# First two token segments of the MLP on whole float32 weights, with the two-part weights made later

## The chip, the cores and the metric

One core of one Trainium2 chip runs the whole program. The metric is the device time in microseconds of one execution. Three runs of the kernel before gave 595.78, 596.35 and 597.09 us; the median, 596.35 us, is the time before.

## The reference, cut to what matters

```python
state = 0                                       # one 48x48 state for each of 4 batches x 8 heads
for t in range(768):                            # gated linear attention
    state = alpha[t][:, None] * state + outer(k[t], v[t])
    y[t] = q[t] @ state
x = y as (3072 tokens, 384)
h = x @ w_in                                    # 384 -> 2048
P = a[0] + a[1]*h + a[2]*h**2 + a[3]*h**3
Q = 1 + abs(b[0])*abs(h) + abs(b[1])*h**2
out = (P / (Q + 1e-6)) @ w_out                  # 2048 -> 384
```

All inputs and the output are float32, except that both weight matrices arrive as float64 words, which the kernel itself turns into float32.

## The kernel before, in words

**Attention.** The 3072 tokens are cut into 12 segments of 256 tokens; a segment is two chunks of 128. Each chunk has two pieces (four heads each), so there are 48 pieces. Gates go through scans on VectorE (`suffix`, L389; `prefix`, L404), products on GpSimd (L418, L422), scores on TensorE (`sc_mm`, L447), evacuation on ScalarE (L456), mask on GpSimd (L460), output and state update on TensorE (`attn_mm`, L490 and L510). The output of a chunk, transposed, is the MLP's input x: ScalarE writes its rounded part (`x_hi`, L535) and VectorE the rest (`x_lo`, L540).

**MLP.** Its columns are cut into 8 units of 256 features. One *job* is one unit of one segment: 96 jobs, numbered u. The first 16 jobs belong to segments 0 and 1 (`NB0 = 2`): units 0 to 5 of segment 0 (u = 0 to 5), the same of segment 1 (6 to 11), then units 6 and 7 of each (12 to 15). From u = 16 on a segment's 8 jobs follow one another. A job does the first product (`mlp_in`, L565, into one of three PSUM banks), the rational function (ScalarE L572 to L595, GpSimd L581, VectorE L585 `t2`, L589, L599, L602, L608), the split of its result g into a rounded part gh (ScalarE, L611) and the rest gl (L615: VectorE for u below 8, GpSimd after), and the second product (`mlp_out_hi`, L626; `mlp_out_lo`, L636) into PSUM banks that collect a segment's output. The product of job u waits for g of job u - 3, whose bank it takes.

**Products in parts.** TensorE multiplies in the type float32r, whose operands are rounded. To keep the accuracy, each operand is a rounded part plus the rest, and three products are added: hi x hi, hi x lo, lo x hi. So a job's first product is 18 matmuls of 256 columns and its second 12 of 384.

**Weights.** There are 16 weight blocks ("keys"): a w_in and a w_out block for each unit. Each arrives as 768 KB of float64 words (`load_w`). ScalarE takes the absolute value of the high words (`join_abs`, L229), VectorE does three integer steps (`join_sign` L234, `join_low` L238, `join` L244), which leave the float32 block in a buffer of the ring wr; ScalarE rounds it (`split_hi`, L253), and the rest is taken from it (`split_lo`, L260) on VectorE for units 0 to 3 and on GpSimd for units 4 to 7. The first product of a job waits for `split_lo` of its w_in block.

**What sets the order.** Every step is registered with an engine, a cost and the steps that it needs; the planner's costs only served a search. The program is written out in the order of the list `ORDER`, a compressed permutation of the steps, and each engine runs its own steps strictly in that order. The planner's costs of the matrix products (1.08 us for half of `mlp_in`, 0.72 us for half of `mlp_out_hi`) are the same before and after.

Of the kernel before, what the change touches and what calls it, by code (L numbers as in the profile page):

```python
# [12 lines left out]
F32 = mybir.dt.float32  # L13
# [9 lines left out]
class Plan:  # L23
# [30 lines left out]
    'c-jTQ17IC65CG7-OD>n>Z)=BkUfbEWZQHhO+qP}nwr$(C-<t`cFcOBsR2T)(Au^1GVK5OKguplehz1iV3PgpNFrI>8',  # L54
    'Gz7scSPH`-28@ANFbx#Mh7m9xmcU$?1j}FoY=L>O80NzQ*bb{;Hf)5Iuo^bNbXWs(U@c6f888`Ez#`ZSQ(!ABhlQ{U',
    'w!scK4eJ46IqigXkP$Y)3W@{qVGW&v&9IW<!ag_*YiSiF27>*tj&{RpiU%8M4;+BwkO|gPD%eC@=m>0Ao9QTQpaif(',
    'ZKq=}iMG-X3WH*h1a{F*+D759o6f-*$N^{J0;Gn6u!l~<71*gJ(=K%g&ckzc0;)g+yigY*AsnDfP!=x3UV5cos%!98',
    'U4?yA8{Vnc>KGlSG>{1L!x2gfIpHWJgO-pMl0$b$2Pq&Iq=%Hy2r|G=RRA(WaVQACR6oc9x#5q>3LW6L0==L9D%5Y(',
    'LCOZ%;W)ilAJifGr^-PjeS)UYN3~m>p~#x_Cv}PTD5V9?(`OZ=E!+dGPf`?ZAez2F55WWLQ*@DTKy)3fPm|F%;fpE{',
    'XG!#Z_^K+vJGe}R-~;ScS177JM|a_y+NZv&!Vp8>f*&eGSA^?O1f0$TURQ!UP!#gQBM8-%A%T7mF?E=J47VX4)PeNc',  # L60
    'pw;0zgO1R3L1PI>r~|qlJb+9(u}-9`0^<|NsOy8r%(^5r0E<a<7VR*WPO7WHTZpYoK{6dz3qFI=5Kjj%xo!wkDTU6e',
    'Q|jkXP`83N@B&^!DqTpY)>U<39Y+_{)gitvqO0jLPy^EF8al1cri<z7x+bL4we?fDLD_XJsG}oe4qaRaVNU%Ta_Pnp',
    '2}|gjItn&{k~+7prAz6b&|Ei#x;h@V(Dn2mh>Ll2OPx>G*RLQx=GUcl9Q+Gq^i@(AfPYX{x7PRQ3pCI@bvfNeU!zaZ',
    'Q1{Y}bb0*|n!#w@M}LOAx;c!|fUR@^-CMWSEnuwfulwp>&`w{caIBy^!T?=SBevIJ7!@n&4mtu`!%eEJJL*VKMYn;k',
    '&_p-ZKcJ~@3*&S%{T({#e!3k@)Zbvd?yTFxK%D?5>A8B44#q6lMbFcN^#t7mGT?9MrswOPkPy4;$$E$;oT3xqP`yz1',
# [71 lines left out]
TB = 3  # L137
# [6 lines left out]
def tile_gla_then_rational_mlp(ctx, tc, q, k, v, alpha, w_in, w_out, ca, cb, out):  # L144
# [413 lines left out]
    def h_of(u):  # L558
        return bank(u % 3)
# [420 lines left out]
```

## Time and profile before

| what | value |
|---|---|
| median of three runs | 596.35 us |
| the profiled execution's own time | 596.56 us |
| its span, first to last instruction | 594.9 us |
| TensorE busy | 537.8 us (90% of the span) |
| VectorE busy | 501.2 us (84%) |
| ScalarE busy | 472.8 us (79%) |
| GpSimd busy | 389.2 us (65%) |
| mean granted TensorE clock | 0.970 |

In the profile PE is TensorE, PEld its weight loads, DVE VectorE, ACT ScalarE, POOL GpSimd and SP the queue that issues the DMAs. Busy time is the union of an engine's instructions; records of neighbours on DVE overlap by some hundredths of a microsecond. "L585" is a line of the kernel. Since busy shares are means over the span, the span has to be cut into stretches; the marks used here are the starts of `t2` (L585), the first VectorE step of each job.

### The profile page before, as it was taken

How to read it: one execution, taken by the hardware profiler on the slowest of the kernel's cores; microseconds unless marked ns; L12 is line 12 of the kernel's file. 1: busy time of each engine (PE TensorE's matmuls, PEld its weight loads, DVE VectorE, ACT ScalarE, POOL GpSimd, SP SyncE). 2: the span in 40 equal slices, each digit the busy share in tenths (PEclk: the TensorE clock that was granted, in tenths of full speed). 3: DMA queues.
4: the chain of work that ended last, by engine and by line, in shares of the span. 5: the costliest groups of instructions: out<-in, count | busy, mean ns of one | idle time of the engine just before them, and what ended most of it. 6: DMA issues, size and time to landing. Idle time of an engine off the chain costs nothing.

```text
span 594.9 us, 14103 instructions
## 1 busy us (share of the span) xinstructions
PE 537.8 (90%) x5362; PEld 502.8 (85%) x5362; DVE 501.2 (84%) x782; ACT 472.8 (79%) x803; POOL 389.2 (65%) x422
## 2 busy tenths in 40 slices
PE   3965765989989999999999999999999999999995
PEld 2644655878879999999999999899999999999994
DVE  4379999999999989998887989999899788758872
ACT  3555775767968988989898988999997987878882
POOL 4543454658787778777766676787767586655562
PEclk9986889889999999999999999999999999999998
DMA  9998431233325334344412444344402000000000
GB/s 170 216 363 327 56 39 23 35 45 49 53 32 127 48 67 84 51 66 70 83 24 57 81 91 72 49 76 81 77 29 42 14 28 2 2 28 1 28 2 32
DMA packets 179979, 41.91 MB, mean 70 GB/s; under 512 B 169408, under 2 KB 172480, under 8 KB 179904
## 3 DMA queue, kind: packets, MB, share of 16 engines
q1 hardware_dynamic: 179904, 40.94, 34.9%
q8 instruction: 44, 0.72, 0.5%
q14 instruction: 31, 0.25, 0.1%
HBM read 36.18 MB, written 4.72 MB: 69 GB/s over the span
## 4 chain that ended last, share of the span: by engine, by line
PE 72%; DVE 12%; SPq 5%; ACT 4%; DMA 4%; issue 2%; DVEq 0%; ACTq 0%
PE ps L565 31%; PE ps L626 19%; PE ps L636 10%; PE ps L490 6%; PE ps L447 5%; SPq L331 2%; SPq L356 2%; DMA wo_words<-in_moe_w_out_dram 2%; DVE wo_words L238 1%; DVE t L599 1%; DVE ps L602 1%; DMA wr<-in_alpha_dram 1%; DVE t L608 1%; DVE t L585 1%; PE ps L510 1%
## 5 line engine op out<-in xcount | busy, mean ns | idle before, releaser
L565 PE MATMUL ps<-x,wi 128*128 128x256 f32 x1728 | 231.3, 289 | 22.8 <-DVE t L608 10.7
L565 PEld LDWEIGHTS ps<-x,wi 128*128 128x128 f32 x1728 | 220.9, 195 | 32.0 <-DVE t L608 13.5
L626 PE MATMUL ps<-wo,gh 128*128 128x384 f32 x768 | 158.0, 343 | 8.9 <-ACT gh L611 5.1
L581 POOL TENSOR_TENSOR qm<-qm,ah 128x512 f32<-128x512 f32 x96 | 127.9, 1334 | 57.5 <-ACT qm L578 56.6
L615 POOL TENSOR_TENSOR gl<-t,gh 128x512 fp32r<-128x512 f32 x88 | 117.1, 1332 | 54.2 <-ACT gh L611 26.3
L626 PEld LDWEIGHTS ps<-wo,gh 128*128 128x128 f32 x768 | 132.4, 190 | 13.9 <-ACT gh L611 5.8
L575 ACT ACTIVATE t<-ps,coef 128x512 f32<-128x512 f32 x96 | 74.2, 773 | 18.5 <-PE ps L565 10.8
L585 DVE TENSOR_TENSOR t<-t,ps 128x512 f32<-128x512 f32 x96 | 65.2, 680 | 27.1 <-ACT t L575 18.8
L599 DVE SCALAR_TENSOR_TENSOR t<-t,coef,ps 128x512 f32<-128x512 f32 x96 | 70.6, 737 | 18.7 <-ACT ps L595 18.2
L636 PE MATMUL ps<-wo,gl 128*128 128x384 f32 x384 | 83.1, 338 | 1.8 <-DVE gl L615 1.8
L578 ACT ACTIVATE qm<-ah,bab 128x512 f32<-128x512 f32 x96 | 78.1, 814 | 6.1 <-DVE ps L602 3.8
L592 ACT ACTIVATE ps<-qm,one_eps 128x512 f32<-128x512 f32 x96 | 66.0, 688 | 15.9 <-DVE t L589 8.6
L589 DVE SCALAR_TENSOR_TENSOR t<-t,coef,ps 128x512 f32<-128x512 f32 x96 | 70.6, 740 | 2.9 <-ACT ah L572 1.1
L636 PEld LDWEIGHTS ps<-wo,gl 128*128 128x128 f32 x384 | 67.8, 188 | 2.4 <-DVE gl L615 2.3
L572 ACT ACTIVATE ah<-ps 128x512 f32<-128x512 f32 x96 | 56.9, 594 | 15.7 <-PE ps L565 13.8
L611 ACT ACTIVATE gh<-t 128x512 fp32r<-128x512 f32 x96 | 60.2, 627 | 10.7 <-DVE t L608 10.3
L608 DVE SCALAR_TENSOR_TENSOR t<-ps,t 128x512 f32<-128x512 f32 x96 | 65.9, 687 | 2.3
L602 DVE SCALAR_TENSOR_TENSOR ps<-qm,ps 128x512 f32<-128x512 f32 x96 | 65.9, 686 | 0.0
L595 ACT ACTIVATE ps<-ps 128x512 f32<-128x512 f32 x96 | 56.0, 584 | 1.8
L447 PE MATMUL ps<-tq,tk 48*128 48x192 f32 (+1 forms) x384 | 44.3, 349 | 1.1 <-POOL tq L422 1.1
L460 POOL TENSOR_SCALAR_AFFINE_SELECT sc<-sc 128x512 f32<-128x512 f32 x48 | 33.4, 697 | 18.0 <-ACT sc L456 17.8
L456 ACT ACTIVATE sc<-ps 128x768 f32<-128x768 f32 (+1 forms) x48 | 37.0, 773 | 5.5 <-PE ps L447 3.2
(94 smaller groups left out, 591.6 us busy)
## 6 DMA issues: line engine op xcount, KB each, us to landing
wi_words<-in_moe_w_in_dram SPq DMA_DIRECT2D x8, 768.0 KB, 10.3
wo_words<-in_moe_w_out_dram SPq DMA_DIRECT2D x8, 768.0 KB, 10.1
tv<-in_v_dram SPq DMA_DIRECT2D x24, 192.0 KB, 3.1
out_dram<-parts SPq DMA_DIRECT2D x24, 192.0 KB, 2.2
wr<-in_alpha_dram SPq DMA_DIRECT2D x18, 256.0 KB, 2.9
raw_q<-in_q_dram SPq DMA_DIRECT2D x80, 32.0 KB, 2.1
raw_a<-in_alpha_dram SPq DMA_DIRECT2D x80, 32.0 KB, 2.1
raw_k<-in_k_dram SPq DMA_DIRECT2D x80, 32.0 KB, 2.0
```

The lines of the kernel that those rows point to most:

```text
L447: nc.tensor.matmul(bank(home(i) + j)[:, SW * a : SW * a + w], tk[n % NQ][r, c, :], tq[n % NQ][r, c, 0:w], start=True, stop=True,)
L565: nc.tensor.matmul(h_of(u)[:, ff * SEG : (ff + 1) * SEG], split_w["i", j][:, kt * FU + ff, w, :], x[:, kt, xp, :], start=(kt == 0 and n == ...
L575: nc.scalar.activation(buf(s, "t1", u), h_of(u), AF.Identity, bias=a2, scale=a3)
L578: nc.scalar.activation(buf(s, "qm", u), buf(s, "ah", u), AF.Identity, bias=b0, scale=b1)
L581: nc.gpsimd.tensor_tensor(buf(s, "qm", u), buf(s, "qm", u), buf(s, "ah", u), op=ALU.mult)
L585: nc.vector.tensor_tensor(t, t, h_of(u), op=ALU.mult)
L599: nc.vector.scalar_tensor_tensor(t, t, a0, h_of(u), op0=ALU.add, op1=ALU.mult)
L602: nc.vector.scalar_tensor_tensor(h_of(u), buf(s, "qm", u), 1.0 + 1e-6, h_of(u), op0=ALU.add, op1=ALU.mult)
L608: nc.vector.scalar_tensor_tensor(t, h_of(u), 2.0, t, op0=ALU.subtract, op1=ALU.mult)
L615: (nc.vector if GL_DVE[0] <= u < GL_DVE[1] and s is fast_bufs else nc.gpsimd).tensor_tensor(buf(s, "gl", u).rearrange("p a b -> p (a b)"), ...
L626: nc.tensor.matmul(o_of(tt), buf(s, "gh", u)[:, ff, tt * P : (tt + 1) * P], split_w["o", j][:, ff, w, :], start=(j == j0 and ff == 0 and w ...
L636: nc.tensor.matmul(o_of(tt), buf(s, "gl", u)[:, ff, tt * P : (tt + 1) * P], split_w["o", j][:, ff, 0, :], start=False, stop=(j == j1 and f ...
```

## The change

For segments 0 and 1 (jobs 0 to 15) the MLP multiplies whole float32 operands: x is written once, as float32, without `x_lo`; the weight block after `join` is copied as it is (`keep`, ScalarE) over the words; `mlp_in` is 6 matmuls instead of 18, `mlp_out_hi` takes g itself (the buffer t1) in 4 matmuls, and gh, gl and `mlp_out_lo` are gone. A job's t1 therefore now waits for the second product of job u - 3. From job 16 on the products are as before. For that the two parts of each block are made later: after the last of the 16 jobs that uses the block, a DMA on the SP queue brings the copy back into a buffer of wr (`bring`, 384 KB, SBUF to SBUF), then `split_hi` (ScalarE) and `split_lo`, now on VectorE for all 16 blocks, write both parts over the copy. `ORDER` is another permutation. The diff without the list:

```diff
-LO_DVE = (0, 4)
+LO_DVE = (0, 8)
...
-    def split_hi(key):
+    def keep(key):
         kind, j = key
         n = P if kind == "i" else DM
         rf = split_w[key][2].bitcast(F32).rearrange("p (a n) -> p a n", n=n)
-        t = weights.tile([P, FU * DM // n, 2, n], F32R, tag=f"w{kind}{j}", name=f"w{kind}{j}")
+        t = weights.tile([P, FU * DM // n, 2, n], F32, tag=f"w{kind}{j}", name=f"w{kind}{j}_whole")
+        nc.scalar.activation(t[:, :, 0, :], rf, AF.Copy)
+        split_w[key] = t
+    def bring(key, n):
+        t = split_w[key]
+        nc.sync.dma_start(wr[n % WB].bitcast(F32).rearrange("p (a n) -> p a n", n=t.shape[3]), t[:, :, 0, :])
+    def split_hi(key, n):
+        kind, j = key
+        w = P if kind == "i" else DM
+        rf = wr[n % WB].bitcast(F32).rearrange("p (a n) -> p a n", n=w)
+        t = weights.tile([P, FU * DM // w, 2, w], F32R, tag=f"w{kind}{j}", name=f"w{kind}{j}")
         nc.scalar.activation(t[:, :, 0, :], rf, AF.Copy)
         split_w[key] = (t, rf)
...
+            if plain:
+                nc.tensor.matmul(
+                    h, split_w["i", j][:, kt * FU + ff, 0, :], x[:, kt, 0, :],
+                    start=(kt == 0), stop=(kt == KT - 1),
+                )
+                continue
...
+            if s is fast_bufs and m < NB0:
+                nc.tensor.matmul(
+                    o_of(tt), buf(s, "t1", u)[:, ff * SEG + tt * P : ff * SEG + (tt + 1) * P],
+                    split_w["o", j][:, ff, 0, :],
+                    start=(j == j0 and ff == 0), stop=(j == j1 and ff == FU - 1),
+                )
+                continue
...
-        add(("hi", key), "ACT", 0.85, split_hi, (key,), [("join", key)])
+        add(("keep", key), "ACT", 0.85, keep, (key,), [("join", key)])
+        user = max(u for u, x in enumerate(jobs) if x[0] < NB0 and x[1] == key[1])
+        add(("bring", key), "SP", DMA, bring, (key, n), [("keep", key), ("in" if key[0] == "i" else "oh", user, 1)]
+            + [("keep", x) for i, x in enumerate(keys) if wr_slot(i) == n % WB] + [("lo", x) for x in keys[:n][-WB:][:1] if n >= WB], kb=1.5)
+        add(("hi", key), "ACT", 0.85, split_hi, (key, n), [("bring", key)])
...
-        add(("xl", g), "DVE", 0.55, x_lo, (g,), [("xh", g)])
+        if m >= NB0:
+            add(("xl", g), "DVE", 0.55, x_lo, (g,), [("xh", g)])
...
-                [("xl", 2 * m), ("xl", 2 * m + 1), ("lo", ("i", j)), ("in", u, 0) if ff else ("in", u - 1, FU - 1), ("g", u - 3)]
+                [(w, 2 * m + x) for w in ("xh", "xl") for x in range(2)]
+                + [("keep" if m < NB0 else "lo", ("i", j)), ("in", u, 0) if ff else ("in", u - 1, FU - 1), ("g", u - 3)]
...
-        add(("t1", u), "ACT", 0.78, act_t1, (u, fb), ins + [("gl", u - TB), ("gh", u - TB), "coef"])
+        add(("t1", u), "ACT", 0.78, act_t1, (u, fb), ins + [("gl", u - TB), ("gh", u - TB), "coef"] + ([("oh", u - TB, 1)] if u >= TB and jobs[u - TB][0] < NB0 else []))
...
-            add(("gh", u), "ACT", 0.64, act_gh, (u, fb), [("g", u), ("ol", u - GB)])
+        if m >= NB0:
+            add(("gh", u), "ACT", 0.64, act_gh, (u, fb), [("g", u), ("ol", u - GB)])
```

What the two lists say when they are unpacked, for the instructions between the same steps:

| stretch | VectorE, before | VectorE, after | TensorE, before | TensorE, after |
|---|---|---|---|---|
| t2 of job 0 to t2 of job 16 | 7 `split_lo`, 8 gl, 4 `x_lo`; 14 each of sign, low, join | 3 `split_lo`, no gl, 2 `x_lo`; 13 sign, 13 low, 14 join; 2 fewer L380, 1 fewer L383, 1 more L389, 2 more L646 | 8 output steps of attention, 9 score steps | 9 and 10 |
| t2 of job 16 to t2 of job 28 | no `split_lo` | 13 `split_lo`; 1 more L599, L602, L608 and `x_lo`; 2 more L380 and L383 each; 2 fewer L646, 1 fewer L389 and L386 | 7 and 7 | 7 and 6 |
| t2 of job 28 to t2 of job 48 | 21 jobs' steps | 20 jobs' steps | 10 and 9; 43 halves of `mlp_out_hi`, 21 `mlp_out_lo` | 8 and 9; 40 and 19 |

## Rows read from the trace of the kernel before

**Rows 1.** The page: busy time, and TensorE in 40 slices.
```profile
PE 537.8 (90%) x5362; PEld 502.8 (85%) x5362; DVE 501.2 (84%) x782; ACT 472.8 (79%) x803; POOL 389.2 (65%) x422
...
PE   3965765989989999999999999999999999999995
```

**Rows 2.** Timeline of DVE (start, duration): t2 of jobs 0, 16 and 28.
```profile
42.03 0.69 DVE L585 TENSOR_TENSOR t<-t,ps 128x512 f32<-128x512 f32 x1 [1.25 <-ACT ah L572]
...
170.64 0.69 DVE L585 TENSOR_TENSOR t<-t,ps 128x512 f32<-128x512 f32 x1 [0.54 <-ACT t L575]
...
232.22 0.69 DVE L585 TENSOR_TENSOR t<-t,ps 128x512 f32<-128x512 f32 x1 [0.53 <-ACT t L575]
```

**Rows 3.** Windows: length; busy (x) of PE, PEld, DVE, ACT, POOL; PEclk; DMA; GB/s.
```profile
140.30:170.60 30.30, 26.05 (x262) 23.84 (x259) 29.00 (x45) 22.44 (x37) 22.81 (x21) 1.00 0.31 44
42.00:170.60 128.60, 95.46 (x914) 86.81 (x915) 123.63 (x178) 90.41 (x137) 71.71 (x73) 0.89 0.39 82
170.60:232.20 61.60, 61.15 (x663) 57.40 (x662) 56.36 (x95) 53.49 (x92) 48.94 (x55) 1.00 0.42 78
232.20:344.10 111.90, 111.90 (x1144) 106.79 (x1144) 97.02 (x156) 99.96 (x176) 79.94 (x83) 1.00 0.36 62
```

**Rows 4.** The chain that ended last, in order of time: start, length, what.
```profile
74.86 0.94 DVE wi L260
...
124.59 0.61 DVE t L608
```

**Rows 5.** Timeline of DVE: two `split_lo` one behind the other.
```profile
51.11 0.94 DVE L260 TENSOR_TENSOR wi<-parts,wi 128x768 fp32r<-128x768 f32 x1
51.98 0.94 DVE L260 TENSOR_TENSOR wo<-parts,wo 128x768 fp32r<-128x768 f32 x1
```

**Rows 6.** L615 and L260 in 42 to 170.6 us: busy (x) on DVE and POOL.
```profile
42.00:170.60 128.60, 5.51 (x8) 8.32 (x6) 0.89 0.39 82
...
42.00:170.60 128.60, 7.28 (x7) 15.66 (x8) 0.89 0.39 82
```

**Rows 7.** Instructions by line and shape, whole span: busy us, mean ns, idle before.
```profile
L540 DVE TENSOR_TENSOR x<-ps,x 128x384 fp32r<-128x384 f32 x24 | 13.2, 549 | 4.6 <-ACT x L535 4.4
L253 ACT ACTIVATE wi<-wr 128x768 fp32r<-128x768 f32 x6 | 5.0, 837 | 0.1
L611 ACT ACTIVATE gh<-t 128x512 fp32r<-128x512 f32 x96 | 60.2, 627 | 10.7 <-DVE t L608 10.3
```

**Rows 8.** The same view, 42 to 170.6 us: the step `join_low`.
```profile
L238 DVE SCALAR_TENSOR_TENSOR wo_words<-wo_words 128x768 uint32<-128x768 uint32 x7 | 9.8, 1405 | 0.0
```

**Rows 9.** Timeline of PE, a stretch at full clock: start, duration, instructions.
```profile
227.35 0.62 PE L490 MATMUL ps<-sc,tv 128*32 128x128 f32 x16
227.79 0.35 PE L510 MATMUL ps<-tv,sc 128*32 128x48 f32 x16
228.07 0.92 PE L447 MATMUL ps<-tq,tk 48*128 48x192 f32 x8
228.92 2.39 PE L565 MATMUL ps<-x,wi 128*128 128x256 f32 x18
231.15 1.55 PE L626 MATMUL ps<-wo,gh 128*128 128x384 f32 x8
232.53 0.86 PE L636 MATMUL ps<-wo,gl 128*128 128x384 f32 x4
233.32 0.65 PE L490 MATMUL ps<-tq,st_d 128*32 128x128 f32 x16
```

**Rows 10.** The page's DMA issues: count, KB each, us from issue to landing.
```profile
wi_words<-in_moe_w_in_dram SPq DMA_DIRECT2D x8, 768.0 KB, 10.3
...
wr<-in_alpha_dram SPq DMA_DIRECT2D x18, 256.0 KB, 2.9
```

**Rows 11.** Timelines of POOL and DVE: a POOL step, a `join_sign` under it.
```profile
84.95 1.80 POOL L260 TENSOR_TENSOR wi<-wr,wi 128x768 fp32r<-128x768 f32 x1
...
85.04 2.15 DVE L234 TENSOR_SCALAR wo_words<-wo_words 128x768 uint32<-128x768 uint32 x1
```

More of the change, by code (lines that the diff above doesn't have):

```diff
@@ L529, in tile_gla_then_rational_mlp, with x_of @@
     XB = NXB
-    xts = ring("x", XB, [P, KT, 2, SEG], F32R)
+    xts = {}
+    def x_of(m):
+        if m not in xts:
+            xts[m] = work.tile([P, KT, 2, SEG], F32 if m < NB0 else F32R, tag=f"x{m % XB}", name=f"x{m}")
+        return xts[m]
     def x_hi(g):
         m, cc = divmod(g, 2)
-        o = xts[m % XB][:, :, 0, cc * C : (cc + 1) * C]
+        o = x_of(m)[:, :, 0, cc * C : (cc + 1) * C]
         nc.scalar.activation(o, bank(3, DM).rearrange("p (k t) -> p k t", t=C), AF.Copy)
@@ L559, in h_of, with mlp_in @@
         return bank(u % 3)
-    def mlp_in(u, ff, x):
+    def mlp_in(u, ff, x=None):
         m, j, _, _ = jobs[u]
+        h = h_of(u)[:, ff * SEG : (ff + 1) * SEG]
+        plain = x is None and m < NB0
+        x = x_of(m) if x is None else x
         for kt in range(KT):
+            if plain:
[4 more added lines that the diff above has]
+                continue
             for n, (w, xp) in enumerate(((0, 0), (0, 1), (1, 0))):
                 nc.tensor.matmul(
-                    h_of(u)[:, ff * SEG : (ff + 1) * SEG], split_w["i", j][:, kt * FU + ff, w, :],
+                    h, split_w["i", j][:, kt * FU + ff, w, :],
                     x[:, kt, xp, :], start=(kt == 0 and n == 0), stop=(kt == KT - 1 and n == 2),
@@ L798, in tile_gla_then_rational_mlp @@
             at=W_ACT.get(key[1], 0.0))
-        add(("abs", key), "ACT", 0.91, join_abs, (key, n), [("w", key)] + [("lo", x) for i, x in enumerate(keys[:n]) if wr_slot(i) == wr_slot(n)][-1:])
+        add(("abs", key), "ACT", 0.91, join_abs, (key, n), [("w", key)] + [("keep", x) for i, x in enumerate(keys[:n]) if wr_slot(i) == wr_slot(n)][-1:])
         add(("sign", key), "DVE", 0.55, join_sign, (key,), [("abs", key)], lock=True)
@@ L871, in tile_gla_then_rational_mlp @@
             [("sm", i), ("d", i), ("am", i - 1), ("v", g), "set_st"]
-            + ([("xl", g - 1)] if gq == 0 else [])
+            + ([("xl", g - 1), ("xh", g - 1)] if gq == 0 else [])
             + [("cp", *key, x) for key in nat_users[3] for x in range(2) if i < 2], lat=0.13, due=due)
@@ L916, in tile_gla_then_rational_mlp @@
             add(("oh", u, ff), "PE", 0.72, mlp_out_hi, (u, ff, fb),
-                [("gh", u), ("lo", ("o", j)), ("oh", u, 0) if ff else ("ol", u - 1)] + old, due=at + ff)
-        add(("ol", u), "PE", 0.72, mlp_out_lo, (u, fb), [("oh", u, 1), ("gl", u)], lat=0.13, due=at + 2)
+                ([("g", u), ("keep", ("o", j))] if m < NB0 else [("gh", u), ("lo", ("o", j))])
+                + [("oh", u, 0) if ff else ("ol", u - 1), ("oh", u - 1, 1)] + old, due=at + ff)
+        if m >= NB0:
+            add(("ol", u), "PE", 0.72, mlp_out_lo, (u, fb), [("oh", u, 1), ("gl", u)], lat=0.13, due=at + 2)
         if j == j1:
@@ L922, in tile_gla_then_rational_mlp @@
                 if j0:
[L923 removed]
+                    add(("dn", u, tt), "DVE", 0.5, mlp_done, (u, tt, fb), [("ol", u), ("oh", u, 1), ("dn", ends[m], tt)], due=at + 3)
                 else:
[L925 removed]
+                    add(("dn", u, tt), "ACT", 0.49, mlp_done, (u, tt, fb), [("ol", u), ("oh", u, 1)] + old + [("keep", x) for i, x in enumerate(keys) if wr_slot(i) >= WB], due=at + 3)
                 if j1 == NU - 1:
```

145 lines of the change are left out of this document (72 added, 73 removed).

## The prediction

> **What bounds the kernel now.** The page comes first: TensorE is busy for 90% of the span, but its slices are full only from about the 13th of 40 on [rows 1]. So the kernel has two halves, and I cut the span at the first VectorE step of jobs 0, 16 and 28, at 42.0, 170.6 and 232.2 us [rows 2], and asked the windows for each stretch. In A, 42.0 to 170.6 us (the first 16 jobs, those that the change rewrites), VectorE is busy for 123.6 of 128.6 us, 96%, TensorE for 95.5 at a mean granted clock of 0.89, GpSimd for 71.7 [rows 3]. The chain of waits says the same: from 74.9 to 125 us nearly all its pieces are VectorE's [rows 4]. In B, to 232.2 us, TensorE is busy for 61.2 of 61.6 us and VectorE for 56.4: TensorE sets the pace, VectorE has 9% left. In C, to 344.1 us, TensorE is busy for all of 111.9 us [rows 3], and the slices stay full to the end. So a microsecond of VectorE work counts in A, one of TensorE work counts in B and C, and what is put into B must fit into VectorE's 5 us of idle time there.
>
> **A, VectorE.** The eight gl go: 5.5 us [rows 6]. Seven `split_lo` become three; two in a row start 0.87 us apart [rows 5], so -3.5. Two `x_lo` go, 0.55 each [rows 7]: -1.1. Of the steps that only the order moves, five leave A and three come in; at some 0.6 us each (my estimate, by the `x_lo` row) -1.2. Together -11.3: 112.3 us.
>
> GpSimd loses its eight `split_lo`, 15.7 us, and six gl, 8.3 us, a third of its 71.7 [rows 3, 6]. That matters to VectorE, since some of its steps stand still under a GpSimd step: `join_low` takes 1.41 us on average for one kind of block [rows 8], where a `split_lo` of the same size takes 0.94 [rows 5], and a `join_sign` that began under a 1.80 us GpSimd step took 2.15 [rows 11]. Seven `join_low` lose 3.3 us so; with the other locked steps perhaps 6. A third of that gone is -2, bounds 0 and -6. VectorE: 110.3 us.
>
> **A, TensorE.** Here the change costs. No float32 product of this shape is in the trace; the nearest are those of the attention. `sc_mm` asks for four matmuls and the row shows eight instructions [rows 9], so a float32 matmul is two. Sixteen instructions of 128 columns, which lie four side by side in the array, take 0.44 us from start to start (227.35 to 227.79) [rows 9]: four in sequence, 0.11 us each, 0.86 ns a column. By that a job's first product is 12 instructions of 0.22 us, 2.64, its second 8 of 0.33, 2.64. Now the first takes 2.23 us (228.92 to 231.15) and the second 2.17 (to 233.32) [rows 9]. So +0.41 and +0.47 a job, 14 us over sixteen jobs. The bounds: at the pace of the float32r instructions, 0.124 and 0.173 us each, a job would save 1.5 us; by the score row, 0.85 us for four in sequence of 192 columns, 1.1 ns a column, it would lose 2.4. I take 0.86 ns, since that row holds the steady pace and the score row also a start. In A: 15 first products +6.2, 13 second +6.1, and the order brings one more output and score step, +1.6 (227.35 to 228.92): 95.5 becomes 109.4 us. Job 0's first product lies ahead of 42 us and shifts the start by about half a microsecond, which the missing `x_lo` in front of it gives back: nothing.
>
> **A, its length.** Both engines now need 110 us. VectorE alone, at the 96% that it holds now, would take 115; but each now waits for the other, and I allow 5 us more: 120, **8.6 us less**. Jobs stay coupled, since the product of job u waits for g of job u - 3.
>
> **A, what else.** ScalarE: `keep` (16, as dear as `split_hi`, 0.84) stands where `split_hi` stood, and gh (0.63) goes [rows 7]; nothing, ScalarE is busy for 90 of 128.6 us [rows 3]. The new wait of t1 for the second product of job u - 3 holds ScalarE's queue, with ah, q1 and the square steps of other jobs behind it, and then t2 on VectorE; in the new order that product stands ahead of, or one product behind, the first product of job u, so the wait is bounded by one 2.64 us product. It is in the 5 us.
>
> **B.** Thirteen `split_lo` come in, 13 x 0.87 = 11.3 us, and the order puts eight small steps in and four out, +2.4: VectorE 56.4 becomes 70.1 us. TensorE: 61.2 and three second products more, 62.6; it no longer binds. ScalarE has 13 `split_hi` more, 10.9: 64.4. At 96%, VectorE's share in A, B takes 72.8 us: **11.2 us more**.
>
> `bring` is not in the trace. The nearest rows are loads of 256 KB, which land after 2.9 us, and of 768 KB, after 10.3, many of them queued at once [rows 10]. I take 3.5 us for 384 KB, nearer the first. A slot of the ring then needs 3.5 + 0.84 + 0.87 = 5.2 us a block, 42 us for its eight, and there are eleven jobs for it, over 60 us: hidden. At 10.3 us it would be 96 and late by 30; what hides it is gone from some 5.8 us a landing on. On the SP queue the 16 DMAs, each with a wait for a product, `split_lo` or both, stand in front of loads of later segments, whose next users are the VectorE transposes; B's VectorE backlog covers these. Nothing.
>
> **C.** TensorE binds. The new order has two attention outputs (1.2 us each: 0.72 from 227.35 to 228.07, and 0.44 for the state part) and 1.5 second products fewer in C, done earlier: -6.0, of which one output comes back later, +1.2: **4.8 less**. Nothing after that changes in amount.
>
> **The sum**: -8.6 + 11.2 - 4.8 = -2.2 us on the profiled execution's 596.56 (span 594.9 and 1.7 around it), 594.4; that execution is 0.2 above the median of 596.35, so **594.2 us**. The VectorE work up to job 28 is nearly the same as before (about -1 us of it), so the change postpones more than it removes; what it can win is idle time.
>
> **Rivals.** *TensorE decides A (slower).* Outside its own stretches TensorE was never busier than 86%, in 140.3 to 170.6 us [rows 3]; if it stays so, 109.4 us of work take 127 and A wins 1.4 us only. Then -1.4 + 11.2 - 4.8 = +5.0: 601.4. It decides once A is longer than 122.2 us, that is once TensorE's share stays below 90%. For it: three banks couple the engines, and the granted clock in A is 0.89. Against it: a TensorE with more to do waits less and so keeps its clock, and it reaches 99% in B beside a VectorE at 91%.
>
> *The moved `split_lo` stand under GpSimd.* In B GpSimd is busy 79% of the time with steps of 0.89 us on average (48.94 over 55) [rows 3]. If each of the 13 waits for what runs, 0.79 x 0.45 = 0.35 us, B grows by 4.6: 598.8. Against it: the seven in A took 7.28 us, 1.04 each, 0.1 more than their 0.94 [rows 5, 6], with GpSimd at 56%, since the order sets them apart. The Trainium skill, "SBUF — State Buffer", section "Who interferes with whom", has the rule behind it: a VectorE instruction with two SBUF inputs and a GpSimd one that reads SBUF exclude each other, and the later one blocks for the whole of the other; the pair in [rows 11] agrees.
>
> *Both stretches pack tightly (faster).* If TensorE's added work fills only its idle time, A takes VectorE's 115 (-13.6), and B at 99% 70.8 (+9.2): with C -9.2, 587.2. For it: VectorE ran almost without a gap from 74.9 to 125 us; against it: it had TensorE waiting for it then.
>
> **Chances.** The forecast 0.42, with a range of its own from 591 to 597; TensorE decides 0.28; GpSimd 0.12; tight packing 0.18. A difference of about 0.2%, 1.2 us, is what a measurement of this kernel can tell. Faster: 0.30 of the forecast and the tight packing, 0.48; same: the forecast's other 0.12; slower: the two others, 0.40. The range reaches from just below the tight packing to 1.6 us above the dearest rival, 586 to 603; late `bring` landings and the high bound of the float32 price lie beyond it.
>
> **What would show it.** In the changed profile: L565 and L626 in jobs 0 to 15 as two instructions a matmul, 0.22 and 0.33 us apart; t2 of job 16 at about 162 us, t2 of job 28 at about 235; VectorE busy near 96% between these two, with TensorE idle for some 10 us there; `bring` landing in 3 to 4 us; `join_low` nearer 0.94 us. Wrong would be: t2 of job 16 later than 165 (TensorE decides), `split_lo` above 1.2 us (GpSimd), TensorE waiting for the two parts of a block while VectorE is idle (late landings), or instructions of 0.12 us (float32 cheaper than I take it, and everything some 20 us earlier in A).

## The result, and the profile after

Four runs of the changed kernel gave 589.73 to 591.57 us, median 590.05; the kernel before gave 596.72 beside them (four runs, 595.78 to 597.09). The ratio is 0.9896 [0.9874, 0.9917]: some 6.5 us faster, where 2.2 were forecast. The profiled execution took 589.73 us, its span is 587.7.

The page of the changed kernel, the lines that answer to [rows 1], with the clock's line and the issues of `bring` and of the word loads:

```profile
PE 546.9 (93%) x5202; PEld 487.3 (83%) x5202; DVE 501.0 (85%) x778; ACT 478.3 (81%) x803; POOL 365.9 (62%) x406
...
PE   4776989999997999999999999999999999999996
...
PEclk9987999999999999999999999999999999999999
...
wi_words<-in_moe_w_in_dram SPq DMA_DIRECT2D x8, 768.0 KB, 7.6
...
wr<-wi_whole SPq DMA_DIRECT2D x8, 384.0 KB, 2.9
wr<-wo_whole SPq DMA_DIRECT2D x8, 384.0 KB, 2.8
```

VectorE's total is what it was (501.2, now 501.0 us), as the prediction had it, and TensorE's is 9.1 us higher; TensorE's slices are now full from about the fifth on. The marks of [rows 2], t2 of jobs 0, 16 and 28, now on L613 (timeline of DVE):

```profile
41.28 0.69 DVE L613 TENSOR_TENSOR t<-t,ps 128x512 f32<-128x512 f32 x1 [2.86 <-ACT t L603]
...
151.97 0.68 DVE L613 TENSOR_TENSOR t<-t,ps 128x512 f32<-128x512 f32 x1
...
227.57 0.69 DVE L613 TENSOR_TENSOR t<-t,ps 128x512 f32<-128x512 f32 x1 [0.84 <-ACT ah L600]
```

The windows of the changed kernel, columns as in [rows 3]: A cut at job 4, all of A, then B, C and the rest:

```profile
41.30:75.70 34.40, 27.24 (x280) 20.35 (x277) 32.82 (x51) 28.23 (x40) 15.48 (x25) 0.90 0.77 218
75.70:152.00 76.30, 73.91 (x493) 53.03 (x492) 73.09 (x113) 57.25 (x88) 33.51 (x41) 1.00 0.43 78
...
41.30:152.00 110.70, 101.16 (x772) 73.38 (x769) 105.91 (x163) 85.48 (x127) 48.98 (x66) 0.97 0.54 121
152.00:227.60 75.60, 68.50 (x724) 61.20 (x723) 72.69 (x114) 62.38 (x102) 44.67 (x45) 1.00 0.47 112
227.60:330.20 102.60, 102.30 (x991) 97.33 (x990) 92.25 (x146) 93.65 (x166) 77.78 (x77) 1.00 0.41 71
330.20:587.70 257.50, 248.12 (x2457) 235.35 (x2455) 207.70 (x328) 216.42 (x370) 168.61 (x164) 0.99 0.19 38
```

And those windows of the kernel before that [rows 3] does not have:

```profile
42.00:90.30 48.30, 30.05 (x328) 27.23 (x329) 46.37 (x65) 32.58 (x46) 19.93 (x25) 0.80 0.54 152
90.30:170.60 80.30, 65.41 (x588) 59.58 (x587) 77.26 (x114) 57.83 (x91) 51.79 (x48) 0.95 0.29 39
...
344.10:594.90 250.80, 242.07 (x2381) 231.53 (x2379) 203.79 (x322) 208.74 (x360) 166.37 (x161) 0.99 0.20 38
```

| stretch | before | after | change | forecast |
|---|---|---|---|---|
| A, jobs 0 to 15 | 128.6 | 110.7 | -17.9 | -8.6 |
| of it up to t2 of job 4 | 48.3 | 34.4 | -13.9 | |
| B, jobs 16 to 27 | 61.6 | 75.6 | +14.0 | +11.2 |
| C, jobs 28 to 47 | 111.9 | 102.6 | -9.3 | -4.8 |
| the rest | 250.8 | 257.5 | +6.7 | 0 |

With 0.7 us of an earlier start these make the span's 7.2 us. The shape is the forecast's: won in A, most of it given back in B. C and the rest belong together: TensorE is busy for 9.6 us less in C (111.90 to 102.30) and 6.1 us more behind it (242.07 to 248.12), so two thirds of what left C was only done later.

Cutting A at job 4 shows more than A as a whole. Three quarters of the gain lie in the first four jobs, where VectorE was busy 96% of the time before and is 95% now, with 13.6 us less to do. From job 4 on the two engines have changed places: TensorE is busy for 73.91 of 76.30 us, 97%, at a clock of 1.00, VectorE for 96%. The chain that ended last, in order of time, says it too. Before, it lay with VectorE only from 75 to 125 us (41.6 of these 50.1 us) [rows 4]. Ahead of that it passed over VectorE, TensorE and the issues of the SP queue in turn, and from 125 us to job 16 it was mostly TensorE's, 33.8 of 45.6 us, beginning with this first product:

```profile
125.25 3.92 PE ps L565 x18
```

Now it is a load of weight words first, and from 61 us on almost only products, 81.2 of 90.7 us (L654 the whole second, L587 the whole first):

```profile
42.60 13.52 DMA wi_words<-in_moe_w_in_dram
...
61.36 2.20 PE ps L654 x6
63.56 2.59 PE ps L587 x12
66.15 2.58 PE ps L654 x8
68.73 5.19 PE ps L587 x24
...
112.33 5.16 PE ps L654 x16
```

The price of a whole float32 product stands in the same lines: 2.59 us for the 12 instructions of a first one, 0.216 each, 2.58 for the 8 of a second, 0.323 each.

VectorE's integer steps became faster. By line and shape, the kernel before in A, beside the `join_low` of [rows 8] (7 of them, 9.8 us):

```profile
L238 DVE SCALAR_TENSOR_TENSOR wi_words<-wi_words 128x768 uint32<-128x768 uint32 x7 | 7.8, 1121 | 0.0
L234 DVE TENSOR_SCALAR wo_words<-wo_words 128x768 uint32<-128x768 uint32 x7 | 5.5, 782 | 0.1
L234 DVE TENSOR_SCALAR wi_words<-wi_words 128x768 uint32<-128x768 uint32 x7 | 5.0, 726 | 0.0
```

and the changed kernel in A (41 to 156 us), with the scan that an experiment below will slow down, and the two groups of `split_lo` in B:

```profile
L238 DVE SCALAR_TENSOR_TENSOR wo_words<-wo_words 128x768 uint32<-128x768 uint32 x7 | 6.8, 974 | 0.0
L403 DVE TENSOR_TENSOR_SCAN tg<-ta,ones 128x516 f32<-128x516 f32 x5 | 6.1, 1225 | 0.0
L238 DVE SCALAR_TENSOR_TENSOR wi_words<-wi_words 128x768 uint32<-128x768 uint32 x6 | 5.7, 954 | 0.0
...
L234 DVE TENSOR_SCALAR wo_words<-wo_words 128x768 uint32<-128x768 uint32 x7 | 4.1, 604 | 0.0
...
L234 DVE TENSOR_SCALAR wi_words<-wi_words 128x768 uint32<-128x768 uint32 x6 | 3.4, 566 | 0.1
...
L274 DVE TENSOR_TENSOR wo<-wr,wo 128x768 fp32r<-128x768 f32 x7 | 7.7, 1102 | 0.0
L274 DVE TENSOR_TENSOR wi<-wr,wi 128x768 fp32r<-128x768 f32 x6 | 6.7, 1117 | 0.0
```

28 steps took 9.8 + 7.8 + 5.5 + 5.0 = 28.1 us; 26 now take 20.0, which for 28 would be 21.5. So 6.6 us of standing still are gone, where the prediction took 2 and gave 6 as the bound.

Which GpSimd steps they had stood still under can be read in the kernel before. Eight of the 28 steps took at least 0.3 us longer than their kind does undisturbed, 7.3 us together, and each overlaps a GpSimd step. Only one of the eight, the pair of [rows 11], stood under work that the change takes away (1.6 us). The others stood under steps that both kernels have, mostly the product qm (L581), such as this `join_low` behind it (timelines of POOL and DVE):

```profile
46.21 1.96 POOL L581 TENSOR_TENSOR qm<-qm,ah 128x512 f32<-128x512 f32 x1
...
46.97 2.01 DVE L238 SCALAR_TENSOR_TENSOR wo_words<-wo_words 128x768 uint32<-128x768 uint32 x1
```

So, as far as the trace shows, most of it went because other steps now stand beside each other; only about a fifth had been held up by the GpSimd work that is gone.

### The profile page after: what moved, and what is told of

Read it like the earlier page. It is cut to its first block, busy times and chain, and to the rows that moved or that the text cites. A ratio compares the mean times of both kernels' runs of the same rounds, so it can differ in the third digit from the quotient of the medians.

```text
span 587.7 us, 13758 instructions
## 1 busy us (share of the span) xinstructions
PE 546.9 (93%) x5202; PEld 487.3 (83%) x5202; DVE 501.0 (85%) x778; ACT 478.3 (81%) x803; POOL 365.9 (62%) x406
## 4 chain that ended last, share of the span: by engine, by line
PE 62%; DVE 13%; ACT 9%; DMA 6%; issue 3%; POOL 3%; SPq 3%; ACTq 0%; DVEq 0%; POOLq 0%
PE ps L593 21%; PE ps L661 13%; PE ps L654 7%; PE ps L671 6%; PE ps L587 6%; PE ps L504 4%; PE ps L461 4%; DMA wi_words<-in_moe_w_in_dram 2%; DVE t L613 2%; DMA wo_words<-in_moe_w_out_dram 2%; DVE t L636 2%; DVE ps L630 2%; ACT t L603 2%; DVE t L627 2%; DVE t L617 1%
## 5 line engine op out<-in xcount | busy, mean ns | idle before, releaser
L593 PE MATMUL ps<-x,wi 128*128 128x256 f32 x1440 | 187.6, 283 | 5.7 <-DVE t L636 4.9
L593 PEld LDWEIGHTS ps<-x,wi 128*128 128x128 f32 x1440 | 179.1, 188 | 12.7 <-DVE t L636 5.8
L643 POOL TENSOR_TENSOR gl<-t,gh 128x512 fp32r<-128x512 f32 x80 | 108.6, 1358 | 59.2 <-ACT gh L639 25.4
L661 PE MATMUL ps<-wo,gh 128*128 128x384 f32 x640 | 130.0, 340 | 4.7 <-DVE wo L274 3.8
L661 PEld LDWEIGHTS ps<-wo,gh 128*128 128x128 f32 x640 | 110.0, 188 | 8.2 <-DVE wo L274 4.6
L613 DVE TENSOR_TENSOR t<-t,ps 128x512 f32<-128x512 f32 x96 | 65.3, 680 | 21.7 <-ACT t L603 16.7
L671 PE MATMUL ps<-wo,gl 128*128 128x384 f32 x320 | 70.0, 340 | 0.0
L639 ACT ACTIVATE gh<-t 128x512 fp32r<-128x512 f32 x80 | 50.2, 628 | 9.5 <-DVE t L636 9.0
L671 PEld LDWEIGHTS ps<-wo,gl 128*128 128x128 f32 x320 | 55.3, 188 | 1.9 <-issue 1.5
L587 PE MATMUL ps<-x,wi_whole 128*128 128x256 f32 x192 | 46.4, 392 | 1.9 <-ACT wi_whole L254 1.4
```

Source lines behind the costliest of these rows:

```text
L587: nc.tensor.matmul(h, split_w["i", j][:, kt * FU + ff, 0, :], x[:, kt, 0, :], start=(kt == 0), stop=(kt == KT - 1),)
L593: nc.tensor.matmul(h, split_w["i", j][:, kt * FU + ff, w, :], x[:, kt, xp, :], start=(kt == 0 and n == 0), stop=(kt == KT - 1 and n == 2),)
L643: (nc.vector if GL_DVE[0] <= u < GL_DVE[1] and s is fast_bufs else nc.gpsimd).tensor_tensor(buf(s, "gl", u).rearrange("p a b -> p (a b)"), ...
L661: nc.tensor.matmul(o_of(tt), buf(s, "gh", u)[:, ff, tt * P : (tt + 1) * P], split_w["o", j][:, ff, w, :], start=(j == j0 and ff == 0 and w ...
L671: nc.tensor.matmul(o_of(tt), buf(s, "gl", u)[:, ff, tt * P : (tt + 1) * P], split_w["o", j][:, ff, 0, :], start=False, stop=(j == j1 and f ...
```

## The experiments

All start from the changed kernel, except the last. The marks of their profiled executions, in us; the ratio is to the kernel before on the same chip. A mark is one execution's: t2 of job 0, ahead of which e4, e7, e8 and e12 change nothing, stands at 40.6 to 41.7 us in them, so a difference of a microsecond says little.

| kernel | median | ratio | t2 of job 16 | t2 of job 28 | span |
|---|---|---|---|---|---|
| changed kernel | 590.05 | 0.9896 [0.9874, 0.9917] | 151.97 | 227.57 | 587.7 |
| e1_pe_more | 597.64 | 1.0012 [0.9993, 1.0030] | 158.85 | 235.53 | 596.0 |
| e9_pe_less | 592.26 | 0.9933 [0.9905, 0.9961] | 149.89 | 227.34 | 590.2 |
| e2_dve_gl | 597.31 | 1.0022 [1.0000, 1.0044] | 156.92 | 232.42 | 592.5 |
| e10_dve_less | 590.44 | 0.9903 [0.9878, 0.9928] | 151.86 | 227.23 | 587.5 |
| e3_pool_lo | 594.50 | 0.9959 [0.9942, 0.9977] | 155.82 | 232.31 | 592.5 |
| e11_tb4 | 589.62 | 0.9883 [0.9858, 0.9908] | 152.29 | 229.04 | 588.4 |
| e4_lo_pool | 591.16 | 0.9906 [0.9889, 0.9923] | 153.11 | 229.71 | 589.8 |
| e8_o_pool | 591.61 | 0.9910 [0.9875, 0.9945] | 151.73 | 227.64 | 590.1 |
| e7_no_lo | 586.12 | 0.9829 [0.9796, 0.9862] | 152.43 | 223.50 | 583.8 |
| e12_bring_twice | 625.02 | 1.0503 [1.0458, 1.0547] | 153.27 | 260.07 | 620.9 |
| e5_old_order | 654.08 | 1.0954 [1.0907, 1.1001] | 202.45 | 290.31 | 652.2 |
| e6_old_work | 626.27 | 1.0491 [1.0453, 1.0529] | 193.08 | 263.08 | 624.1 |

### What sets A

TensorE's side. One whole float32 matmul more in each of the 16 jobs (it starts a group that the next one starts again, so its sum is not used):

```diff
+        if plain and ff == 0:
+            nc.tensor.matmul(h, split_w["i", j][:, ff, 0, :], x[:, 0, 0, :], start=True, stop=True)
```

> The changed kernel with one more whole float32 matmul of 256 columns in each of the first 16 jobs, whose result the next one overwrites: 2 instructions of 0.216 us a job, 6.9 us of TensorE work in all. If VectorE sets the first sixteen jobs, TensorE's idle time there (9.5 us of 110.7) takes it up: 0 to 2 us more than the changed kernel's 590.1. If TensorE sets them: 5 to 7 us more, 595 to 597.

t2 of job 16 is 6.9 us later, just what 16 x 2 x 0.216 us comes to (1.3 of it already at t2 of job 0), and it is never won back: the median is 7.6 us above the changed kernel's. TensorE's work counts in full, or nearly.

One matmul less in each (the first product leaves out one of its six matmuls):

```diff
+                if ff == 0 and kt == KT - 1:
+                    continue
...
-                    start=(kt == 0), stop=(kt == KT - 1),
+                    start=(kt == 0), stop=(kt == KT - 1 - (ff == 0)),
```

> The changed kernel without one of the six whole float32 matmuls of the first product in each of the first 16 jobs (the last 128 of x's features are left out of one half): 0.43 us of TensorE work less a job, 6.9 in all. If TensorE now sets the first sixteen jobs: 4 to 7 us less than 590.1. If VectorE does, or both equally (each holds the other): 0 to 2 us less.

The same 6.9 us taken away bring job 16 only 2.1 us forward, job 28 0.2, and the end not at all: the median is 2.2 us above the changed kernel's, with intervals that overlap, where a shorter time was expected in either case. Up to job 8 it brings 0.3 us (100.97 to 100.63), and from there to job 16 1.7 more.

VectorE's side. Eight idle steps of gl's size, one in each of jobs 0 to 7 (their result is not used):

```diff
+        if u < 8 and s is fast_bufs:
+            nc.vector.tensor_tensor(buf(s, "gl", u).rearrange("p a b -> p (a b)"), t, t, op=ALU.subtract)
```

> The changed kernel with one VectorE subtraction of 128x512 behind g of each of jobs 0 to 7, where before gl stood; its result is not used. Eight times 0.69 us. If VectorE sets the first sixteen jobs: 4 to 6 us more than 590.1, t2 of job 16 later by the same. If TensorE sets them: 0 to 1.5 us more.

They cost 5.5 us of VectorE [rows 6] and put job 4 back by 2.5 us and job 16 by 5.0: VectorE's work counts too, also in the first jobs. (The median is 7.3 us above the changed kernel's, more than the 4 to 6 expected.)

`join_sign` cut to 8 of its 768 words (the signs of the other words are left out):

```diff
-        nc.vector.tensor_scalar(high, high, 0x80000000, None, op0=ALU.bitwise_and)
+        nc.vector.tensor_scalar(high[:, 0:8], high[:, 0:8], 0x80000000, None, op0=ALU.bitwise_and)
```

> The changed kernel with join_sign on 8 of a row's 768 words (the rest keep their exponent bits, so the weights are others): 13 times some 0.5 us of VectorE work less in the first sixteen jobs, 6 to 7 us. If VectorE sets them: 4 to 7 us less than 590.1. If TensorE does: 0 to 2 us less.

VectorE is busy for 101.84 us instead of 105.91 between 41.3 and 152 us, 4.1 less where 6 to 7 were meant; job 16 comes 0.1 us earlier. So in A each engine is nearly as long as the other: to load either costs its full price, to relieve either alone wins almost nothing. In the changed kernel it is TensorE and, ahead of 61 us, the word loads that end last, with VectorE right behind: in e9_pe_less the chain from 61 us to job 16 is VectorE's for 37.0 us and TensorE's for 14.6, in e10_dve_less it stays TensorE's for 82.2 of 90.9.

GpSimd's side. Eight steps without use on GpSimd, each behind the `keep` of a block of units 4 to 7:

```diff
+        if j >= 4:
+            nc.gpsimd.tensor_tensor(t[:, :, 1, :], t[:, :, 0, :], t[:, :, 0, :], op=ALU.subtract)
```

> The changed kernel with one GpSimd subtraction of 128x768 (1.8 us) behind the whole copy of each of the blocks of units 4 to 7, eight in all, as GpSimd made the second parts there before; the result is not used. If GpSimd's steps held up VectorE's in the kernel before: join_low and join_sign grow again (join_low's mean from 0.97 towards 1.2 us), and the run takes 2 to 5 us more than 590.1. If that played no part: 0 to 1 us more.

Nobody waits for these steps, yet job 16 is 3.9 us later and the median 4.5 us higher, as expected; VectorE's busy time up to job 16 grows from 105.91 to 110.59 us. The expected place was missed, `join_low` keeps its 0.95 to 0.98 us; others paid. By line and shape, 41 to 156 us (L405 is the scan L403 of above, L244 is `join`, 0.947 us in the changed kernel for this shape):

```profile
L405 DVE TENSOR_TENSOR_SCAN tg<-ta,ones 128x516 f32<-128x516 f32 x5 | 8.4, 1674 | 0.0
L238 DVE SCALAR_TENSOR_TENSOR wo_words<-wo_words 128x768 uint32<-128x768 uint32 x7 | 6.8, 975 | 0.0
L244 DVE SCALAR_TENSOR_TENSOR wr<-wr,wi_words 128x768 uint32<-128x768 uint32 x5 | 6.0, 1197 | 0.0
...
L234 DVE TENSOR_SCALAR wi_words<-wi_words 128x768 uint32<-128x768 uint32 x6 | 4.2, 703 | 0.1
```

Which step stands still depends on what the order puts beside the GpSimd step; that something does is shown. One of the added steps (L256) and the scan behind it, timelines of POOL and DVE:

```profile
132.64 2.25 POOL L256 TENSOR_TENSOR wo_whole<-wo_whole 128x768 f32<-128x768 f32 x1
...
133.48 2.50 DVE L405 TENSOR_TENSOR_SCAN tg<-ta,ones 128x516 f32<-128x516 f32 x1
```

The scan ends 1.1 us after the GpSimd step, nearly its undisturbed 1.23. The Trainium skill, "SBUF — State Buffer", section "Who interferes with whom", gives the rule, that a VectorE instruction with two SBUF inputs contends with a GpSimd one that reads SBUF, and that the ports they share are an exclusive lock; this scan, with two inputs, agrees.

The new wait of t1, taken away by a fourth buffer:

```diff
-TB = 3
+TB = 4
```

> The changed kernel with four buffers for t1 instead of three, so that t1 of a job waits for the second product of job u - 4, not u - 3; the order is the same. If the new wait costs time in the first sixteen jobs: 1 to 4 us less than 590.1, t2 of job 16 earlier by as much. If the order keeps that product ahead of t1: within 1 us.

The median is 0.4 us lower, job 16 comes 0.3 us later and job 28 1.5: nothing is won. The wait for the second product of job u - 3 costs nothing that can be measured in the new order.

### What sets B

Half the `split_lo` back on GpSimd, by unit and then by kind (w_out blocks only):

```diff
-LO_DVE = (0, 8)
+LO_DVE = (0, 4)
```

> The changed kernel with the second parts of the blocks of units 4 to 7 taken on GpSimd instead of VectorE, in the same places of the order: VectorE has 7 us less to do between jobs 16 and 28, GpSimd some 15 us more. If VectorE's work sets that stretch: 3 to 6 us less than 590.1. If the way from the copy to the second part sets it (each is on time by little, and GpSimd's takes 1.8 us for 0.95): 1 to 5 us more.

```diff
-        eng = nc.vector if LO_DVE[0] <= j < LO_DVE[1] else nc.gpsimd
+        eng = nc.vector if key[0] == "i" else nc.gpsimd
...
-        dve = LO_DVE[0] <= key[1] < LO_DVE[1]
+        dve = key[0] == "i"
```

> The changed kernel with the second parts of the eight w_out blocks on GpSimd, those of w_in on VectorE. The w_out parts are needed some two jobs later than those of w_in of the same unit, so GpSimd's longer step has more time. If GpSimd's 1.8 us just ahead of the product undid the relief of VectorE in the run that moved units 4 to 7: 2 to 5 us less than 590.1. If VectorE's relief is worth nothing in that stretch: 589 to 592.

B in the windows of the two, columns as in [rows 3]; first by unit:

```profile
153.10:229.70 76.60, 71.21 (x724) 63.77 (x723) 64.39 (x105) 62.17 (x102) 61.52 (x53) 0.96 0.47 111
```

then by kind:

```profile
151.70:227.60 75.90, 71.15 (x724) 64.09 (x723) 66.17 (x106) 62.62 (x102) 58.16 (x52) 0.96 0.47 111
```

VectorE has 7 to 8 us less to do there (72.69 to 64.39 and 66.17), and B is 1.0 and 0.3 us longer than its 75.6. So to take work off VectorE is not enough to shorten B. It isn't a clean test of VectorE's sum: the step itself is slower on GpSimd, 1.80 us [rows 11] against 0.95, and TensorE's granted clock is 0.96 in both in place of 1.00, at which the same 724 instructions keep it busy for 71.2 us in place of 68.5.

The step cut to almost nothing (8 columns of each block; the products read the rounded part in place of the rest, so the second parts of the weights are left out):

```diff
-        eng.tensor_tensor(t[:, :, 1, :], rf, t[:, :, 0, :].bitcast(F32), op=ALU.subtract)
+        eng.tensor_tensor(t[:, 0, 1, 0:8], rf[:, 0, 0:8], t[:, 0, 0, 0:8].bitcast(F32), op=ALU.subtract)
...
-                    h, split_w["i", j][:, kt * FU + ff, w, :],
+                    h, split_w["i", j][:, kt * FU + ff, 0, :],
...
-                    split_w["o", j][:, ff, w, :],
+                    split_w["o", j][:, ff, 0, :],
```

> The changed kernel without the second parts of the weights from job 16 on: the step stays in its place and is waited for, but subtracts 8 columns instead of 768, and the products read the rounded part in its stead. VectorE has 13 times some 0.85 us, 11 us, less between jobs 16 and 28, TensorE's work is the same. If VectorE's work sets that stretch: 7 to 11 us less than 590.1. If the waits from step to step set it (as the move of half of the parts to GpSimd, which gave nothing, lets one think): 0 to 4 us less.

```profile
152.40:223.50 71.10, 67.72 (x724) 60.89 (x723) 60.98 (x113) 61.80 (x102) 44.48 (x45) 1.00 0.50 119
```

With 11.7 us less for VectorE in B, B is 4.5 us shorter. TensorE then holds 67.72 of 71.10 us, 95%. So the thirteen steps cost 4.5 us in B, not the 11.3 us of VectorE's time that the prediction counted for them. With TensorE at 95%, little more was to be had.

Every `bring` issued twice:

```diff
-        nc.sync.dma_start(wr[n % WB].bitcast(F32).rearrange("p (a n) -> p a n", n=t.shape[3]), t[:, :, 0, :])
+        for _ in range(2):
+            nc.sync.dma_start(wr[n % WB].bitcast(F32).rearrange("p (a n) -> p a n", n=t.shape[3]), t[:, :, 0, :])
```

> The changed kernel with each bring issued twice, into the same place: 16 more DMAs of 384 KB, and the rounding waits for the second. If the way back of the copies is hidden: within 1.5 us of 590.1. If it is on the path between jobs 16 and 28: 3 to 10 us more.

35 us, far above the 3 to 10 expected, and 31 of them between jobs 16 and 28 (B is 106.8 us). The waits of the SP queue, 116 to 262 us (L261 is `bring`; us in all, times, longest), for the w_out blocks:

```profile
SPq L261 <- DMA wr<-wo_whole: 20.5, 9, 4.3
```

and of ScalarE in the same stretch (L268 is `split_hi`):

```profile
ACT wo L268 <- DMA wr<-wo_whole: 25.1, 8, 6.7
```

For the w_in blocks it is 19.9 and 21.1 us. The second copy waits for the first to land, so each block's way back is a landing longer, and B grows by 31 us for the 13 blocks that are split in it, 2.4 each, most of a landing. So less than a landing of slack is left on this way. Part of the price is not the way's own: the queue issues nothing else while it waits, and the chain of B passes also over loads of the attention's inputs that stand behind it (L346, 14% of B, beside 36% for landings of `bring`); the run does not part the two.

In the changed kernel the way back can be read off directly. Timeline of the SP queue, the last three issues of `bring`:

```profile
190.58 0.60 SPq L260 DMA_DIRECT2D wr<-wo_whole  x1
...
197.11 0.60 SPq L260 DMA_DIRECT2D wr<-wo_whole  x1
...
203.91 0.60 SPq L260 DMA_DIRECT2D wr<-wo_whole  x1
```

and of DVE, the `split_lo` of the last four w_out blocks:

```profile
189.56 0.95 DVE L274 TENSOR_TENSOR wo<-wr,wo 128x768 fp32r<-128x768 f32 x1
...
196.13 0.96 DVE L274 TENSOR_TENSOR wo<-wr,wo 128x768 fp32r<-128x768 f32 x1
...
202.94 0.95 DVE L274 TENSOR_TENSOR wo<-wr,wo 128x768 fp32r<-128x768 f32 x1
...
213.14 2.04 DVE L274 TENSOR_TENSOR wo<-wr,wo 128x768 fp32r<-128x768 f32 x1
```

Each `bring` is issued within 0.1 us of the end of the `split_lo` before it (190.51, 197.09, 203.89): all w_out blocks go through one buffer of wr, and the w_in blocks through the other. From issue to issue it takes 6.5 and 6.8 us: 2.8 for the landing, 0.84 for `split_hi`, 0.95 for `split_lo`, and 2 us of waiting in the queues of ScalarE and VectorE. TensorE waits three times for what comes out, its largest wait in B (waits of PE, 152 to 228 us):

```profile
PE ps L661 <- DVE wo L274: 3.8, 3, 2.9
```

But the last of the `split_lo` above, which is on B's chain just ahead of a second product, took 2.04 us because it began under a GpSimd step of 1.29 us (L643, from 213.07 us). And the landing itself is nearly hidden. ScalarE stands idle for one only three times in B, 2.2 us in all (waits of ACT, the same stretch; L267 is `split_hi`):

```profile
ACT wo L267 <- DMA wr<-wo_whole: 1.5, 2, 0.8
ACT wi L267 <- DMA wr<-wi_whole: 0.7, 1, 0.7
```

No landing is among the pieces of the chain through B: it is VectorE's for 34.8 of 75.6 us, TensorE's for 21.1 and ScalarE's for 11.3. So e12_bring_twice shows how little slack the way back has, and not that it sets B as it is. That the one buffer of each kind does is not shown either: a ring of its own for `bring` was not tried.

### The order

The changed work in the order of before, with `bring`, `split_hi` and `split_lo` behind the same first products as in the new order (diff: the list `ORDER` only):

> The changed kernel's work in the order of the kernel before: the whole copy stands where the rounding stood, the steps that are gone are left out, and the bring, the rounding and the second part of each block come behind the same product steps as in the changed kernel. If the gain is the lighter work of the first sixteen jobs, most of it is still there: 590 to 594 us. If it is the new order's packing, it is gone: 597 to 603.

64 us above the changed kernel, outside both ranges expected; job 16 comes 50 us later. Here the wait of t1 that was free above is dear (waits of ScalarE, 120 to 210 us; L598 is t1, L649 the whole second product):

```profile
ACT t L598 <- PE ps L649: 14.3, 7, 4.0
```

The work of before in the order of after, with each part put behind the step that it needs:

> The kernel before's work (products in three parts, both parts of each block at once) in the changed kernel's order: the rounding and the second part stand where the whole copy stands, gh and gl behind g, the second part of x behind the first. If the gain is the lighter work: at or above the kernel before, 596 to 604. If it is the new order: 590 to 594.

36 us above the changed kernel, again outside both ranges, and 22 us later at job 16 than in its own order. TensorE waits for gh there (waits of PE, 60 to 193 us):

```profile
PE ps L622 <- ACT gh L607: 14.6, 5, 6.5
```

So neither half of the change is worth anything in these two mixtures; each order fits the work that it was searched for. The two runs price a mismatch; they don't divide the 6.5 us between work and order, and how much of it another order could have won with the work of before is not shown.

## Why the prediction was right, and where not

**Direction and range held, and the outline of the mechanism: won in A, given back in B. The size is partly luck.** 590.05 lies within 586 to 603 and a little below the forecast's own 591 to 597; it is 4.1 us from the forecast and 2.9 from the tight packing, a rival. The terms missed by more than their sum: A came out 9.3 us shorter than forecast, B 2.8 longer, C with the rest 2.2 longer. And faster had a chance of only 0.48.

**The float32 price held.** 0.22 and 0.33 us an instruction were taken from an attention row [rows 9]; 0.216 and 0.323 were measured, 2.59 and 2.58 us a product for 2.64. Both bounds were far off.

**A, VectorE: one term mis-sized.** The removed work is as counted; the standing still under GpSimd was taken as -2 and is -6.6, just past its bound. That is the difference between 110.3 us forecast and 105.9 measured. Rows 8 and 11 showed the size; a third of the GpSimd work gone was taken as a third of the blocking gone, and it depends instead on which steps the order puts beside each other: seven of the eight steps held up before stood under GpSimd steps that are still there, and in e3_pool_lo the same GpSimd work put back held up others. The pair of [rows 11] does not bear out the rule given with it in the GpSimd rival, which is for steps with two SBUF inputs: `join_sign` has one and a constant. `join_low`, with two, does (46.97 us, above).

**A, TensorE: the sum took slow microseconds for work.** 109.4 us were forecast, 101.16 measured. The added work is real: busy time multiplied by clock, an estimate, goes from 86.2 to 98.4 us, 12.2 of the 13.9 forecast. But before, up to job 4, TensorE was busy for 30.05 us at a granted clock of 0.80, where it now has 0.90, and from job 4 on 1.00 instead of 0.95. A busy time at a mean clock of 0.89 [rows 3] is no amount of work to add full-speed microseconds to.

**A, its length: "I allow 5 us more" failed.** The prediction took VectorE for the limit of all of A, which the chain bears out only up to 125 us; behind that it was TensorE's already. Two engines with nearly equal work were expected to lose to each other. They take 110.7 us, less even than the tight packing's 115: VectorE keeps its 96% (105.91 of 110.70) beside a TensorE that reaches 97% from job 4 on. That each costs in full when loaded (e1_pe_more, e2_dve_gl) and wins little when relieved (e9_pe_less, e10_dve_less) is the coupling as these runs have it; it was there, but without the 5 us. The new wait of t1, put into them, is nothing (e11_tb4). The rival that TensorE decides A named the engine rightly for the stretch behind job 4, and its share, below 90%, wrongly.

**B: the size was nearly right, the reason half.** VectorE at 96% was forecast and is there, with 72.69 us in place of 70.1: the thirteen `split_lo` take 14.4 us for 11.3, 2 us of it since two stood still for a microsecond each under a GpSimd step (1.94 and 2.04 us: the GpSimd rival, in two of thirteen cases), the rest since records overlap by 0.08 us. TensorE's work was taken as 62.6 us and is 68.5 at a clock of 1.00: the sum added the dearer price of three second products, but not the steps that leave C and are done in B (first products there grow from 198 to 220 instructions). So TensorE's idle time is 7.1 us, forecast some 10, and without the thirteen steps B is only 4.5 us shorter. In "`bring` ... hidden ... Nothing", hidden nearly held for the landing, 2.8 to 2.9 us for the 3.5 taken, and the slot failed: it was counted as 5.2 us a block, without the time that a block waits in two engines' queues; 6.5 to 6.8 is the measure. The slack was overrated too: hiding was to end at some 5.8 us a landing, and two landings in a row, about as much, cost 31 us in e12_bring_twice, though partly by the waiting queue.

**C: "Nothing after that changes in amount" failed.** C won 9.3 us for 4.8, and 6.7 came back behind it. Counted together, -2.6 for -4.8. The term left out the first products: their instructions in C fall from 387 to 363, 1.3 products, some 3 us.

**Still open:** whether B is set by the one buffer of each kind or by VectorE, ScalarE and TensorE in turn. The early arrival at job 16 (2.1 us in e9_pe_less) is lost by job 28, which speaks for a limit inside B; late ones are not made up (6.9 us at job 16 are 8.0 at job 28 in e1_pe_more), so it moves with A when A is late. With the whole work done no run was measurably faster than the changed kernel; the fourth t1 buffer, 589.62 [0.9858, 0.9908], is the same.

## What to carry to other kernels

Cut a stretch again wherever its binding engine may change, and turn busy time at a low granted clock into full-speed time before you add work to it. Where a step stands still under another engine's, look up which step that is before you price its going. Where work is moved to a later stretch, count on every engine what else the order moves there, and follow one item's whole way back (issue, landing, each engine's queue, the buffer that is freed), since the item's throughput, and not the engines' sums, may set the pace. Don't judge a change of work in the old static order: here the same work cost 64 us more in it.

## What the runs showed of the hardware

A float32 matmul is two instructions, and each takes 1.7 to 1.9 times as long as the float32r one at the same clock: 0.216 us against 0.124 for 256 columns, 0.323 against 0.173 for 384. The Trainium skill, "FP8 and Floating Point Precision", section "TensorE Precision Notes", counts four passes for true float32. The whole matmul takes 3.5 and 3.7 times as long as the float32r one here, which is near four if a float32r matmul is one pass; no run here shows that.

A step on GpSimd that nobody waits for isn't free: eight of them without use, 14.1 us of GpSimd, delayed job 16 by 3.9 us through VectorE steps that grew beside them, one kind of scan from 1.23 to 1.67 us.
